# Which of two arena places a set of weight sums is formed in first, and when its stores are issued

## The chip, the core and the metric

The kernel runs on one core of one Trainium2 chip. The core has a matrix engine (PE), a vector engine (DVE), a scalar engine (ACT), a general engine (POOL) and SP, which here only issues DMAs. POOL and ACT issue DMAs too. Each engine runs its own instruction list strictly in order and waits at semaphores for the others; a transfer issued by SP, ACT or POOL goes through that engine's own DMA queue, and all queues share the core's 16 DMA engines.

The metric is the device time of one execution in microseconds (us), as the median over several runs. Beside it stands one execution taken with the hardware profiler, whose trace all readings of engines come from.

## The reference

```python
x = A_x                                            # [1, 2048, 1024] bf16
g = _sigmoid((x * gate_w).sum(-1, keepdims=True))
a = _A_ref(x, A_wqkv, A_wo)     # 32 heads of 32, each position attends to 8 positions, 2 apart
b = _B_ref(x, B_w_gate, B_w_up, B_w_down)          # gelu(x Wg) * (x Wu), 3584 wide, then Wdown
return g * a + (1 - g) * b
...
def _B_ref(x, w_gate, w_up, w_down):
    g = jnp.einsum("bsd,df->bsf", x, w_gate)
    u = jnp.einsum("bsd,df->bsf", x, w_up)
    h = _gelu(g) * u
    return jnp.einsum("bsf,fd->bsd", h, w_down)
```

Almost all work is matrix products: x by the 3072 columns of wqkv, x by 7168 columns of gate and up weights, and the last product, in which the down projection and the attention's output projection are taken together (their rows are stacked).

## The kernel before

**Products by halves.** Every product is done as a 2 by 2 block product with seven block multiplications in place of eight (Winograd's form of Strassen's scheme). That needs sums and differences of the blocks of both factors. They are formed by DVE, in bf16, before PE uses them. For the last product the sums of the right factor (rows of `B_w_down` and `A_wo`, 18 slices of 128 rows by 512 columns for each quarter) are called T1 to T4. They do not fit into the on-chip memory (SBUF) during the first part of the kernel, so they are formed early, in nine *sets* of two slices, and stored to the DRAM tensors `t_d[0..3]`. The last product loads them back from 511 us on.

**One arena.** Nearly all of SBUF is one tile, `arena`, cut by hand into places given in KB of a partition. A place is used for one thing after another. Those that matter here:

- 92 to 108 (`R_W0`): the raw gate and up weights of the first pairs (`raw_ab`), read by PE and by DVE's sums (L327) in the first 24 us. 92 to 100 is later a set's place.
- 56 to 72 (`R_XN`, later `R_PR`): first x as loaded (`xn`, whose second half is 64 to 72), which PE transposes by 16.4 us; later four of the six tiles that take the products of q and k (`prod_tile`, `pr_off = 56, 60, 84, 64, 68, 88`). The diff's title calls 64 to 72 the place of the q-k tiles.
- `R_TF`: where each of the nine sets lies. A set takes 8 KB: four tiles of two slices, `r11, r12, r21, r22`.

**A set's life.** `tf_load(q)` (L873) has SP load the four tiles (eight DMAs of 256 KB for sets 0 and 1 together, L877). `t_forms` (L881) has DVE form the sums in place: one instruction of 128x2048 (L892) gives r11 and r12, and two of 128x1024 (L895) give r22 and then r21. Then POOL issues four stores of 256 KB to `t_d` (L898). Sets 0 and 1 are loaded right behind the kernel's head, ahead of 16 DMA transposes of the second half of x (L1343), all on SP.

**The order of DVE's work.** `t_forms` is a Python generator, one of many background tasks. The main loop goes over *units* b (28 matmuls of 128x512 each, 6.05 us): PE's groups p1, p73 of the unit before, p5, possibly the queued reduces (`slotq`), p26, p4 of the unit before. Between p73 and p4, DVE adds a partial product to two banks (L400) and PE's p4 writes one of them again, so that L400 must end before p4 begins. At the end of a unit `run_bg` spends a budget of about 4.7 us on tasks, by priority: a task is resumed, issues its instructions up to its next `yield`, and the number that it yields is taken off the budget. What a generator holds behind its last `yield` is issued only when it is resumed once more, which may be in a later unit. `t_forms` has the lowest priority of those tasks (6).

**q and k.** From unit Q0 = 2 on, the units are those of q and k. Each stores a part of its result through POOL (L523, L524). Two units later `qk_prods` (L612) forms three product tiles: one DVE instruction of 128x4096 for two tiles (L599) and one of 128x2048 for the third (L592). The first q-k unit's go to 56, 60 and 84, the second's to 64, 68 and 88. PE reduces the six with 24 matmuls (L604). The other lines that come up: L207, the sums of the second half of x, which need the DMA transposes; L245 and L251, a product of gate and up parts and its store by POOL; L289 to L298, the gate's sigmoid, with POOL's load of `zc` and DVE's sum of it (L291).

**POOL's queue.** POOL works off its DMA issues in order. Its DMAs use eight semaphores in turn, so that each issue also waits for the landing of the eighth one before it.

Of the kernel before, what the change touches and what calls it, by code (L numbers as in the profile page):

```python
# [46 lines left out]
R_ST = 178  # L47
R_P5B = 198.5
R_RAW = (0, 8)
R_TF = (92, 64, 100, 108, 92, 16, 92, 100, 108)  # L50
R_S = (16, 24)
R_O = (36, 32)
R_VB = (40, 48.25)
# [9 lines left out]
def _win_ap(src: bass.AP, dims):  # L63
    return AP(src.tensor, src.offset, [list(src.ap[0])] + [list(d) for d in dims])
# [3 lines left out]
def kernel(  # L68
# [12 lines left out]
    nc = tc.nc  # L81
# [24 lines left out]
    def reg3(kb, a, b):  # L106
        return reg(kb, a * b).rearrange("p (a b) -> p a b", a=a)
# [19 lines left out]
    t_d = [tc.dram_tile([P, NK, SC], BF16, name=f"t_d{k}") for k in range(4)]  # L127
# [9 lines left out]
    with tc.manual_schedule(engines={mybir.EngineType.PE, mybir.EngineType.DVE, mybir.EngineType.Activation,  # L137
# [63 lines left out]
        def flat(a):  # L201
            return a.rearrange("p a b -> p (a b)")
# [661 lines left out]
        NP = 2  # L864
# [5 lines left out]
        def tf_set(q):  # L870
            return [reg3(R_TF[q] + NP * k, NP, SC) for k in range(4)]

# [8 lines left out]
        def t_forms():  # L881
            for q in range(NQ):
                tf_q[0] = q
                if q in (N1, N2):
                    tft.prio = 3.9 if q == N1 else 4.5
                    tasks.sort(key=lambda t_: t_.prio)
                while now[0] < (Q0 + (0, 1, 4, 6, 7)[q] if q < N1 else 1 + (TB if q < N2 else TC)):
                    yield None
                r11, r12, r21, r22 = tf_set(q)
                n_ = NP * SC  # L890
                both = _win_ap(flat(r11), [[n_, 2], [1, n_]])
                TT(out=both, in0=_win_ap(flat(r12), [[2 * n_, 2], [1, n_]]), in1=both, op=ALU.subtract)  # L892
                yield 1.14
                for o_, a, b_ in ((r22, r22, r11), (r21, r21, r22)):
                    TT(out=flat(o_), in0=flat(a), in1=flat(b_), op=ALU.subtract)  # L895
                    yield 0.61
                for k, t in enumerate((r11, r22, r12, r21)):
                    nc.gpsimd.dma_start(out=t_d[k][:, NP * q:NP * q + NP, :], in_=t)  # L898

        for q, b in ((2, 2), (3, 4), (4, 5)):  # L900
            at(Q0 + b, lambda q=q: tf_load(q))
        at(TB, lambda: ([tf_load(q) for q in range(N1, N2)], spill_load(1)))
        at(TC, lambda: [tf_load(q) for q in range(N2, NQ)])
        tft = bg(t_forms(), 6, Q0)

        def tf_done():
# [495 lines left out]
```

## Time and profile before

| what | us |
|---|---|
| median of 3 runs (lowest, highest) | 718.88 (717.62, 720.47) |
| the profiled execution | 717.67 |
| its span, first to last instruction | 715.8 |
| PE busy in the span | 705.9 |
| DVE busy | 671.6 |
| ACT busy | 330.0 |
| PE busy in 60 to 72 us | 10.18 of 12 |
| DVE busy in 50 to 60 us | 5.24 of 10 |
| mean share of the DMA engines busy in 50 to 60 us | 1.04 |
| granted TensorE clock | 1.00 throughout |

The span is cut into instructions of each engine; "busy" is the sum of their durations. In a time line each row is one instruction, or some alike in a row (x4): start, length, engine, line, operation, output and inputs; in brackets, the engine's idle time just before and what ended it. The share of the DMA engines is a mean over 16 and can read a little over one.

### The profile page before, as it was taken

Reading aid. Unit: us, or ns where it says so; the run is one execution under the profiler, and the core shown is the slowest. Engines: PE = TensorE matmul, PEld = TensorE weight load, DVE = VectorE, ACT = ScalarE, POOL = GpSimd, SP = SyncE. Lnnn points to the kernel's source line nnn. Section 1 sums busy time; section 2 is a strip of 40 time slices with the busy share of each in tenths; the row PEclk is TensorE's granted clock in tenths of the full one; section 3 lists DMA queues with packets and bytes.
Section 4 is the critical chain, followed back from the end, with each engine's and each line's share of the span. In section 5 each row is a group of like instructions: output and inputs, shape, how many; then the busy total and the mean of one; then the engine's idle time right before and its main releaser. Section 6 shows DMA issues by size and latency. Waiting matters only on the chain.

```text
span 715.8 us, 10650 instructions
## 1 busy us (share of the span) xinstructions
PE 705.9 (99%) x4033; PEld 407.7 (57%) x4089; DVE 671.6 (94%) x631; ACT 330.0 (46%) x602; POOL 143.9 (20%) x248
## 2 busy tenths in 40 slices
PE   9999999999999999999999999999999999999998
PEld 4465656655544444444444444444447886758887
DVE  3997989989999999999999999999699899799997
ACT  5554446445466565555555555555322321132431
POOL 1243544322512332121300010101110002100011
PEclk9999999999999999999999999999999999999999
DMA  9979352384484768665763763464950799995951
GB/s 300 320 197 294 135 177 65 97 239 141 143 278 145 246 206 250 207 218 182 235 180 105 264 208 126 159 261 137 423 241 36 298 397 399 412 430 232 396 215 60
DMA packets 94755, 162.03 MB, mean 226 GB/s; under 512 B 23680, under 2 KB 71200, under 8 KB 90352
## 3 DMA queue, kind: packets, MB, share of 16 engines
q1 hardware_dynamic: 77632, 105.46, 42.9%
q0 software_dynamic: 16352, 48.29, 19.5%
q10 hardware_dynamic: 720, 7.60, 2.7%
q8 instruction: 32, 0.52, 0.3%
q14 instruction: 19, 0.16, 0.1%
HBM read 112.17 MB, written 54.14 MB: 232 GB/s over the span
## 4 chain that ended last, share of the span: by engine, by line
PE 91%; DVE 3%; DMA 3%; issue 2%; POOL 0%; ACT 0%; DVEq 0%; POOLq 0%
PE banks L354 62%; PE banks L1073 19%; PE banks L1106 7%; PE banks L604 2%; DMA h_d<-arena 1%; DMA arena<-h_d 1%; DVE arena L400 1%; PE banks L150 0%; DMA gblk<-g_d 0%; DVE arena L314 0%; DVE arena L774 0%; DVE arena L768 0%; ACT arena L224 0%; POOL gblk L305 0%; PE banks L218 0%
## 5 line engine op out<-in xcount | busy, mean ns | idle before, releaser
L354 PE MATMUL banks<-arena 128*128 128x512 bf16 x2191 | 484.9, 379 | 4.7 <-DVE arena L400 1.5
L354 PEld LDWEIGHTS <-arena 128*128 128x128 bf16 x2240 | 245.8, 110 | 241.6 <-issue 8.2
L1073 PE MATMUL banks<-arena 128*128 128x256 bf16 x1260 | 138.3, 273 | 0.0
L1073 PEld LDWEIGHTS <-arena 128*128 128x128 bf16 x1260 | 123.3, 98 | 15.2 <-issue 0.3
L381 ACT COPY arena<-banks 128x512 f32<-128x512 f32 x80 | 46.9, 587 | 129.8 <-PE banks L354 129.8
L400 DVE TENSOR_TENSOR arena<-banks,arena 128x1024 bf16<-128x1024 f32 x80 | 97.4, 1219 | 8.9 <-ACT arena L408 3.6
L362 ACT CAST arena<-banks 128x512 bf16<-128x512 f32 x104 | 60.9, 585 | 44.1 <-PE banks L354 43.8
L768 DVE TENSOR_TENSOR arena<-arena 128x4096 bf16<-128x4096 bf16 (+1 forms) x40 | 73.5, 1859 | 0.3
L774 DVE TENSOR_TENSOR arena<-arena 128x2048 bf16<-128x2048 bf16 (+2 forms) x53 | 68.0, 1282 | 1.0
L251 POOL DMA_DIRECT2D h_d<-arena x28 | 20.4, 731 | 216.0 <-DVE arena L245 142.1
L1106 PE MATMUL banks<-arena 128*128 128x512 bf16 x281 | 62.6, 379 | 0.5
L389 ACT COPY banks<-banks 128x512 f32<-128x512 f32 x80 | 45.6, 570 | 23.3 <-PE banks L354 20.1
L1031 DVE TENSOR_TENSOR arena<-arena 128x2304 bf16<-128x2304 bf16 x40 | 53.3, 1352 | 0.5
L599 DVE TENSOR_TENSOR arena<-arena 128x4096 bf16<-128x4096 bf16 x22 | 50.1, 2284 | 3.9 <-DMA t_d<-arena 3.8
L376 ACT COPY banks<-banks 128x512 f32<-128x512 f32 x80 | 46.1, 576 | 14.1 <-PE banks L354 12.9
L1078 ACT COPY banks<-banks 128x256 f32<-128x256 f32 x60 | 21.4, 356 | 61.7 <-PE banks L1073 61.5
L1106 PEld LDWEIGHTS <-arena 128*128 128x128 bf16 x288 | 28.0, 98 | 34.0 <-DMA arena<-h_d 0.6
L360 ACT ACTIVATE arena<-banks 128x512 bf16<-128x512 f32 x56 | 33.4, 597 | 20.1 <-PE banks L354 20.1
L954 DVE TENSOR_TENSOR arena<-arena 128x2048 bf16<-128x2048 bf16 (+1 forms) x40 | 41.8, 1112 | 0.4 <-DMA arena<-h_d 0.4
L1039 DVE TENSOR_TENSOR arena<-arena 128x2304 bf16<-128x2304 bf16 x28 | 37.7, 1352 | 0.2
L245 DVE TENSOR_TENSOR arena<-arena 128x2048 bf16<-128x2048 bf16 x28 | 34.0, 1216 | 2.8 <-ACT arena L362 2.8
L314 DVE TENSOR_TENSOR arena<-arena 128x1024 bf16<-128x1024 bf16 x56 | 36.1, 686 | 0.5
(92 smaller groups left out, 455.5 us busy)
## 6 DMA issues: line engine op xcount, KB each, us to landing
arena<-t_d SPq DMA_DIRECT2D x8, 2304.0 KB, 10.2
h_d<-arena POOLq DMA_DIRECT2D x28, 512.0 KB, 4.7
arena<-w_c SPq DMA_DIRECT2D x12, 1152.0 KB, 13.5
t_d<-arena POOLq DMA_DIRECT2D x36, 256.0 KB, 5.3
arena<-h_d SPq DMA_DIRECT2D x6, 1536.0 KB, 13.0
arena<-in_B_w_down_dram SPq DMA_DIRECT2D x28, 256.0 KB, 6.1
r_d<-arena ACTq DMA_DIRECT2D x3, 2304.0 KB, 9.0
arena<-r_d SPq DMA_DIRECT2D x3, 2304.0 KB, 14.2
```

Of the source, the lines that this page charges most:

```text
L354: self.pe = nc.tensor.matmul(ps, lhsT=self.L[form](kt), rhs=rhs[:, kt, :], start=(start and kt == 0), stop=(kt == HK - 1), skip_group_chec ...
L362: nc.scalar.copy(out=o_, in_=i_)
L376: nc.scalar.copy(out=self.Y, in_=self.X)
L381: nc.scalar.copy(out=self.p5s, in_=self.V)
L389: nc.scalar.copy(out=self.Z, in_=self.Y)
L400: TT(out=self.T[:, :, c2s], in0=pair, in1=self.p5s.rearrange("p (o n) -> p o n", o=1).to_broadcast([P, 2, SC]), op=ALU.add)
L599: TT(out=dst, in0=_win_ap(q, [[sq, 2], [0, NWIN], [1, AC]]), in1=_win_ap(k, [[sk, 2], [-DIL, NWIN], [1, AC]]), op=ALU.mult)
L768: TT(out=prod2[:, t % 4:t % 4 + m, :], in0=flat(ab).rearrange("p (o n) -> p o n", o=1).to_broadcast([P, m, NWIN * AC]), in1=_win_ap(v[:, t ...
L774: TT(out=h(0) if w > 1 else o_[:, t:t + m, :], in0=h(0), in1=h(1), op=ALU.add)
L1031: TT(out=o_, in0=a, in1=b_, op=op)
L1073: nc.tensor.matmul(c(i, h, j), lhsT=l[:, kt, j * P:(j + 1) * P], rhs=r[:, kt, :], start=False, stop=(kt == KH - 1), skip_group_check=True)
L1106: nc.tensor.matmul(ps, lhsT=L[:, i, j * P:(j + 1) * P], rhs=R[:, i, :], start=(start and q == 0), stop=(q == NK - 1), skip_group_check=not ...
```

## The change

The places of sets 0 and 1 change places in `R_TF`: set 0 now lies at 64 (the q-k tiles' place) and set 1 at 92. And in `t_forms` the four stores of a set are issued directly behind its last difference, ahead of the last `yield` of the generator's round and not behind it.

```diff
-R_TF = (92, 64, 100, 108, 92, 16, 92, 100, 108)
+R_TF = (64, 92, 100, 108, 92, 16, 92, 100, 108)
...
                 for o_, a, b_ in ((r22, r22, r11), (r21, r21, r22)):
                     TT(out=flat(o_), in0=flat(a), in1=flat(b_), op=ALU.subtract)
+                    if o_ is r21:
+                        for k, t in enumerate((r11, r22, r12, r21)):
+                            nc.gpsimd.dma_start(out=t_d[k][:, NP * q:NP * q + NP, :], in_=t)
                     yield 0.61
-                for k, t in enumerate((r11, r22, r12, r21)):
-                    nc.gpsimd.dma_start(out=t_d[k][:, NP * q:NP * q + NP, :], in_=t)
```

The instruction lists of PE, DVE, ACT and SP keep their order. On POOL, the four stores of set 0 come ahead of the q and k stores of the first q-k unit (they were behind them, behind the load of `zc` and behind two stores of L251), and those of set 1 come to where those of set 0 were, ahead of the second unit's q and k stores. The stores of sets 2 to 8 stay where they were in POOL's list. Which semaphores are waited for changes with it, for the same data.

## The prediction

> **What bounds the kernel now.** I read the page's first part, then the waits, then the stretch of time in which the change acts on PE, DVE, POOL and the SP queue.
>
> ```profile
> span 715.8 us, 10650 instructions
> PE 705.9 (99%) x4033; PEld 407.7 (57%) x4089; DVE 671.6 (94%) x631; ACT 330.0 (46%) x602; POOL 143.9 (20%) x248
> ```
>
> PE is busy all but 9.9 us, and the chain that ended last is 91% PE. Only what fills an idle stretch of PE can pay. The list of waits (us in total, times, longest) has one DVE wait on a DMA and two on which PE pays for a late DVE:
>
> ```profile
> DVE arena L599 <- DMA t_d<-arena: 3.8, 1, 3.8
> PE banks L354 <- DVE arena L400: 1.5, 2, 1.2
> PE banks L604 <- DVE arena L592: 0.5, 1, 0.5
> ```
>
> The time line of DVE (start, length, instruction, idle before and its releaser) shows where the first lies:
>
> ```profile
> 49.01 0.19 DVE L291 TENSOR_REDUCE zs<-zc 128x8 f32<-128x32 f32 x1
> ...
> 53.54 1.23 DVE L400 TENSOR_TENSOR arena<-banks,arena 128x1024 bf16<-128x1024 f32 x1 [1.00 <-PE banks L354]
> 54.68 0.23 DVE L296 TENSOR_SCALAR go<-zs 128x8 bf16<-128x8 f32 x2
> 58.67 2.29 DVE L599 TENSOR_TENSOR arena<-arena 128x4096 bf16<-128x4096 bf16 x1 [3.76 <-DMA t_d<-arena]
> 60.88 1.22 DVE L592 TENSOR_TENSOR arena<-arena 128x2048 bf16<-128x2048 bf16 x1
> 62.02 1.22 DVE L207 TENSOR_TENSOR arena<-arena 128x2048 bf16<-128x2048 bf16 x1
> 63.15 1.22 DVE L400 TENSOR_TENSOR arena<-banks,arena 128x1024 bf16<-128x1024 f32 x1
> ...
> 70.60 1.22 DVE L400 TENSOR_TENSOR arena<-banks,arena 128x1024 bf16<-128x1024 f32 x1
> ```
>
> The L599 at 58.67 writes the second q-k unit's products to the place of set 1, so it waits until set 1 is stored. Everything behind it on DVE is late, and PE's time line shows the bill:
>
> ```profile
> 60.27 1.36 PE L604 MATMUL banks<-arena,ones_r 128*32 128x512 bf16 x20
> 62.15 0.40 PE L604 MATMUL banks<-arena,ones_r 128*32 128x512 bf16 x4 [0.52 <-DVE arena L592]
> 62.48 8.14 PE L354 MATMUL banks<-arena 128*128 128x512 bf16 x35
> 71.87 4.48 PE L354 MATMUL banks<-arena 128*128 128x512 bf16 x20 [1.25 <-DVE arena L400]
> ```
>
> Why the store is late is on POOL's time line: set 0 (L898, four stores) goes out at 46.61 though its last difference ended at 41.97, and set 1 only behind the next q and k stores.
>
> ```profile
> 46.61 2.36 POOL L898 DMA_DIRECT2D t_d<-arena  x4
> 49.39 0.55 POOL L523 DMA_DIRECT2D q_d<-arena  x1 [0.42 <-DVE zs L291]
> 49.92 0.54 POOL L524 DMA_DIRECT2D k_d<-arena  x1
> 50.45 0.54 POOL L898 DMA_DIRECT2D t_d<-arena  x1
> 51.56 0.54 POOL L898 DMA_DIRECT2D t_d<-arena  x1 [0.57 <-DMA h_d<-arena]
> 52.43 0.54 POOL L898 DMA_DIRECT2D t_d<-arena  x1 [0.32 <-DMA t_d<-arena]
> 53.30 0.54 POOL L898 DMA_DIRECT2D t_d<-arena  x1 [0.33 <-DMA t_d<-arena]
> ```
>
> The last is issued at 53.30, such stores land in 5.0 to 5.7 us there (the view of t_d in that stretch), and 58.5 is when L599 is let go.
>
> **The change part by part.** No instruction is added or removed, and the order of instructions on PE, DVE, ACT and SP stays. On POOL alone two groups move: set 0's four stores to ahead of the first q and k stores, set 1's to where set 0's were. The later sets keep their places.
>
> *The removed wait.* The place that L599 needs is now set 0's. POOL stood idle from 21.9 to 43.4, so the four stores go out as their DVE results come: from 40.6 (L892 at 39.30 lasts 1.22) to about 42.9. At the longest landing seen for these stores between 46 and 50 (6.4 us) they are home by 49, 6 us before DVE reaches L599 at 54.91. So the 3.76 us go. Each part alone nearly does it: with only the places swapped, set 0 would leave at 46.61 to 48.97 and land by 54.6; with only the stores moved, set 1 would leave from about 46.6 to 49.4 and land by 55.8, a wait of at most 0.9.
>
> *What PE gets of it.* The reduces at 60.27 need L592, which would now end at 58.3. An undisturbed group of 24 such reduces takes 1.41 (the one from 104.44 to 105.85), here 62.48 - 60.27 = 2.21, so 0.80 is gained. The profile calls 0.52 of it idle. For the second gap I walk DVE: after L599 at 54.91, L592 at 57.1, L207 at 58.25, and L400 at 59.4. Its PE input comes one unit (28 matmuls of 0.216, 6.05 us) after the 53.54 of the one before, at 59.6. From one L400 to the next DVE needs 70.60 - 63.15 = 7.45, so the next runs from 67.05 to 68.3. PE wants it where its idle time begins now, 71.87 - 1.25 = 70.62, less the 0.80 already gained: 69.82. It is there 1.5 us ahead, so the 1.25 goes too. Sum: 0.80 + 1.25 = 2.05, with the idle figures 0.52 + 1.25 = 1.77. I take 2.0; bounds 0 and 2.05 of this part.
>
> *The swapped loads on SP.* Set 0's loads now need only xn's second half, free at 16.4 when the transposes on PE end; before they waited for L327 until 22.25. Set 1's take that wait over. No engine gains: the queue is full there (DMA share 1.06 from 18 to 27 us). The four A_wqkv loads ahead end at 28.2 (the last issue at 14.0 and the longest landing, 14.2), and eight loads of 256 KB land behind them from 28.95 to 34.04 whenever they were issued. Set 0 is used at 39.30, set 1 at 45.29, so 5 us cover it. If the earlier 1 MB were served among the A_wqkv loads, it would take 2.7 us at the 385 GB/s of that stretch, and L460 at 31.36 needs the last but one of those; I take nothing. The place at 92 is loaded again for set 4 at 62 to 64 us, long after set 1's stores.
>
> *What stands behind the moved stores on POOL.* Four issues of 0.54 to 0.76 end by 43.7 at the latest against 43.40 for the first q store: up to 0.3 later. Then comes the load of zc, for which DVE waits at L291 (49.01). It landed in 2.9 us; the q store that ran behind four t_d stores took 5.5. Issued at 44.6 to 44.9 it lands between 47.5 and 50.4, so L291 is between on time and 1.4 late. Cover: DVE's 1.00 idle before L400 at 53.54, and the 12 matmuls (2.6 us) between that unit's p73 and its p4 less the 1.23 of L400, together 2.4. So nothing; without that cover 1.4. The second h store waits for set 0's first to land (47 at the latest, 0.9 late), for which no engine waits.
>
> *The shared DMA engines.* The DMA transposes of x run from 28.94 on SP; L207 needs the last. Their steps are 1.3 us, but not the last two:
>
> ```profile
> 48.69 2.87 SPq L1343 DMA_TRANSPOSE arena<-in_A_x_dram  x1
> 51.61 2.96 SPq L1343 DMA_TRANSPOSE arena<-in_A_x_dram  x1
> 54.61 1.31 SPq L877 DMA_DIRECT2D arena<-in_B_w_down_dram  x1
> ```
>
> They were slow while 3 MB of h and t_d stores drained. The last landed at 51.61 + 7.0 = 58.6, 0.4 after DVE could now begin L207, so L207 starts at 58.7 and the next two L400 are 0.25 later than walked; 1.2 of cover is left. The same bytes drain earlier, so I take the landing as unchanged. Bounds: up to 2 us earlier, for the queue had room from 40 on, which gains nothing; or 4.7 later (the last rival).
>
> The Trainium skill speaks against moving stores into the transposes' time: "DMA: Bandwidth & Descriptors", section "Queues, rings and completion order", says that each DMA engine takes turns packet by packet between the queues that have work. The trace agrees with that, by the steps of 2.9 against 1.3. By the rule alone the moved megabyte delays the transposes it now meets, which is the last rival.
>
> Sum: the profiled execution took 717.67 (span 715.8 and 1.87 around it), so 715.7 after it. The runs' median is 718.88, 1.21 above; carried over, **716.9**.
>
> **Rivals.** (a) *The gain is eaten further on*: PE is 2 us ahead, but a later stretch follows something else. For it: DVE is busy 218.2 of 220 us from 260 to 480, and PE waits on L400 again at 248.31 (0.23). Against it: DVE's idle times up to there (1.76 at 150.73, 0.36 at 165.97) wait for PE, so DVE moves along; no later wait of PE is on a DMA. Time 718.9. (b) *It doesn't do what it says*: the wait only changes its releaser, L599 now held for set 0's bytes. That needs landings of 14 us from 40.6; the longest store seen there took 6.4. Also 718.9. (c) *Slower*: the early megabyte stretches the transposes from 41 on and the later two megabytes stretch the last ones as before. 3 MB drained from 45.3 to 58.6, 225 GB/s, so 1 MB is 4.7 us: the last transpose lands at 63.3, L207 holds DVE until then, L400 ends at 65.6 where PE needs it at 63.4 (reduces end at 61.68, eight matmuls), 2.2 lost; the next ends 7.45 later at 73.1 against 69.82 + 2.2, 1.1 more. 3.3 against the 2.05 now: 1.3 slower, 720.2. It decides from a last landing of about 62.0 on; from 60.0 it already costs. Against it: SP's step at 54.61 shows the slowing was there already.
>
> **How the numbers follow.** Forecast 0.66, (a) and (b) together 0.20, (c) 0.09, and 0.05 for a stall that I have not seen, above 722.5. The runs before lie from 717.62 to 720.47, so 0.5% (3.6 us) is what one can tell from no change. The forecast's 2.0 lies inside it: faster by more needs 715.3 or less, which no idle time of PE between 20 and 500 us pays for, only scatter: 0.14. Slower by more: the last case and the end of (c), 0.07. Range: 1.9 below the forecast for scatter, and up to (c): 715.0 to 720.4.
>
> **What would show it.** Right: no wait of L599 on t_d; the reduces near 60.3 in one group of 24 and no idle PE before the L354 that stands at 71.87; set 0's stores from 40.6; L207 near 58.7. Wrong: DVE idle before L291 (zc), or before L207 beyond 60.0 (transposes), or PE's total idle still near 9.9.

## The result and the profile after

The changed kernel takes 715.19 us (median of 7 runs, 714.86 to 716.73) against 717.92 (7 runs, 717.33 to 720.47) for the kernel before, beside which it ran. The ratio is 0.9957, with a 95% interval of 0.9943 to 0.9972: faster by 2.0 to 4.1 us. The forecast was 716.9, a gain of 2.0 on the 718.88 of the three runs known then. The direction and the place were right. The size was too small: the two medians lie 2.7 us apart, and the ratio means 3.1.

The first part of the page of the kernel after:

```profile
span 713.3 us, 10651 instructions
PE 704.4 (99%) x4033; PEld 406.9 (57%) x4089; DVE 671.6 (94%) x631; ACT 329.9 (46%) x602; POOL 143.5 (20%) x248
```

The span is 2.5 us shorter and PE's work is the same. The time line of DVE in the stretch of the change (start, length, instruction, idle before and its releaser):

```profile
49.16 0.21 DVE L291 TENSOR_REDUCE zs<-zc 128x8 f32<-128x32 f32 x1
49.28 2.28 DVE L599 TENSOR_TENSOR arena<-arena 128x4096 bf16<-128x4096 bf16 x1
53.31 1.23 DVE L592 TENSOR_TENSOR arena<-arena 128x2048 bf16<-128x2048 bf16 x1 [1.75 <-DMA h_d<-arena]
54.45 1.22 DVE L400 TENSOR_TENSOR arena<-banks,arena 128x1024 bf16<-128x1024 f32 x1
55.59 0.24 DVE L296 TENSOR_SCALAR go<-zs 128x8 bf16<-128x8 f32 x2
55.73 2.29 DVE L599 TENSOR_TENSOR arena<-arena 128x4096 bf16<-128x4096 bf16 x1
...
59.07 1.22 DVE L207 TENSOR_TENSOR arena<-arena 128x2048 bf16<-128x2048 bf16 x1
60.20 1.22 DVE L400 TENSOR_TENSOR arena<-banks,arena 128x1024 bf16<-128x1024 f32 x1
...
67.65 1.23 DVE L400 TENSOR_TENSOR arena<-banks,arena 128x1024 bf16<-128x1024 f32 x1
```

The wait of the second L599 on t_d is gone: L599 starts at 55.73, not 58.67. But a wait has come that was not there, 1.75 us of the first L592 on an h store. It took the place of the 1.00 us in which DVE had waited for PE. PE's time line:

```profile
60.39 1.48 PE L604 MATMUL banks<-arena,ones_r 128*32 128x512 bf16 x24
61.80 12.31 PE L354 MATMUL banks<-arena 128*128 128x512 bf16 x55
74.04 1.48 PE L604 MATMUL banks<-arena,ones_r 128*32 128x512 bf16 x24
```

The 24 reduces run in one group and no idle time stands before the next 56 matmuls (55 recorded). And POOL's, where set 0 now leaves at 40.93 and set 1 at 46.93:

```profile
40.93 0.57 POOL L898 DMA_DIRECT2D t_d<-arena  x1 [18.92 <-DVE arena L892]
41.66 1.61 POOL L898 DMA_DIRECT2D t_d<-arena  x3 [0.16 <-issue]
...
44.58 0.77 POOL L289 DMA_DIRECT2D zc<-z_d  x1
45.34 1.49 POOL L251 DMA_DIRECT2D h_d<-arena  x2
46.93 0.56 POOL L898 DMA_DIRECT2D t_d<-arena  x1
47.65 1.72 POOL L898 DMA_DIRECT2D t_d<-arena  x3 [0.17 <-issue]
```

zc and the two h stores are issued when they were before, but with 1 MB of set 0 ahead of them in the queue. zc landed in 4.6 us (2.9 before), the h stores in 6.2 and 7.3 (3.8 and 5.3 before).

**Where the time went.** All kernels here issue the same matmuls, so one measure serves for all: the starts of PE's matmuls at a few landmarks. From the second group of reduces to the last product's first matmul (L1106 in the kernel before) there are 434.8 us in both kernels, and from the first L1073 to the last matmul 168.83 and 168.82. Only three stretches differ: up to the first reduces, from the first to the second group of reduces (the *stage*), and the L1106 near 525 us. The stage took 16.01 us and takes 13.65: 2.36 of the 2.5. Another 0.27 was a wait ahead of an L1106 at 526, which the kernel after does not have, and its first reduces begin 0.12 later, from the kernel's head.

### The profile page after: what moved, and what is told of

It reads as the page before. It is cut to its first block, busy times and chain, and to the rows that moved or that the text cites. A ratio compares the mean times of both kernels' runs of the same rounds, so it can differ in the third digit from the quotient of the medians.

```text
span 713.3 us, 10651 instructions
## 1 busy us (share of the span) xinstructions
PE 704.4 (99%) x4033; PEld 406.9 (57%) x4089; DVE 671.6 (94%) x631; ACT 329.9 (46%) x602; POOL 143.5 (20%) x248
## 4 chain that ended last, share of the span: by engine, by line
PE 95%; DVE 3%; issue 1%; DMA 1%; SPq 0%; DVEq 0%
PE banks L354 65%; PE banks L1074 19%; PE banks L1107 9%; PE banks L604 2%; DVE arena L400 1%; DMA arena<-in_A_x_dram 1%; DVE arena L314 0%; DVE arena L774 0%; DVE arena L222 0%; DVE arena L768 0%; PE banks L273 0%; DVE arena L1288 0%; DVE arena L248 0%; DVE arena L892 0%; DVE arena L245 0%
## 5 line engine op out<-in xcount | busy, mean ns | idle before, releaser
L400 DVE TENSOR_TENSOR arena<-banks,arena 128x1024 bf16<-128x1024 f32 x80 | 97.5, 1219 | 7.9 <-ACT arena L408 3.6
L251 POOL DMA_DIRECT2D h_d<-arena x28 | 20.3, 729 | 216.4 <-DVE arena L245 142.6
L376 ACT COPY banks<-banks 128x512 f32<-128x512 f32 x80 | 46.1, 576 | 14.4 <-PE banks L354 13.2
L599 DVE TENSOR_TENSOR arena<-arena 128x4096 bf16<-128x4096 bf16 x22 | 50.1, 2284 | 0.1
```

The lines of the kernel that those rows point to most:

```text
L376: nc.scalar.copy(out=self.Y, in_=self.X)
L400: TT(out=self.T[:, :, c2s], in0=pair, in1=self.p5s.rearrange("p (o n) -> p o n", o=1).to_broadcast([P, 2, SC]), op=ALU.add)
L599: TT(out=dst, in0=_win_ap(q, [[sq, 2], [0, NWIN], [1, AC]]), in1=_win_ap(k, [[sk, 2], [-DIL, NWIN], [1, AC]]), op=ALU.mult)
```

## The experiments

Theory A: PE pays for nothing but how late DVE is behind the second L599. The rivals are named with the runs. The indented passages are what was expected, written before each run.

**1. Each part of the change alone.** The exchange of places without moved stores (swap_only), and the moved stores without the exchange (move_only):

```diff
swap_only, against the kernel before
-R_TF = (92, 64, 100, 108, 92, 16, 92, 100, 108)
+R_TF = (64, 92, 100, 108, 92, 16, 92, 100, 108)
move_only, against the changed kernel
-R_TF = (64, 92, 100, 108, 92, 16, 92, 100, 108)
+R_TF = (92, 64, 100, 108, 92, 16, 92, 100, 108)
```

> Only the two places are exchanged; the stores of a set stay behind the generator's last yield. Theory A (PE pays for nothing but DVE's lateness behind the second L599): L599 finds set 0 stored long before, starts at 54.9, no wait of L592 either, and from PE's first group of 24 reduces (near 60.3) to its second group there are 13.65 us, as in the changed kernel (16.01 before). Span 713.0 to 713.6. Theory B (a part of the gain comes from the stores being issued earlier, on the DMA queues): between 13.65 and 16.01, and a span over 714.

> Only the stores are moved ahead of the last yield; set 0 stays at 92 and set 1 in the q-k tiles' place. Theory A: set 1's stores leave from 46.9 and land by about 56.2, L592 waits some 1.8 us for the h store as in the changed kernel, the second L599 starts at 55.7 to 56.4, early enough (up to 56.5) for PE not to wait: 13.65 us between the two groups of reduces, span 713.0 to 713.7. Theory B: a part of the gain only, span over 714.

Measured: swap_only 715.34 us (6 runs), ratio 0.9955 (0.9944 to 0.9967), span 713.3, stage 13.65. move_only 716.45 us (12 runs), ratio 0.997 (0.9956 to 0.9984), span 714.6, stage 14.11. So the exchange alone did all of it in this execution, as theory A had it. Two things were closer than expected: L592 waited 0.81 us for h, and set 0's last store landed at 54.80, only 0.2 us ahead of L599 (55.02). move_only fell short of it. Its stage and span are what theory B had, but theory B's reason, stores that go out earlier, is ruled out by swap_only, which moves no store and has all of the gain. The DVE of move_only shows another reason:

```profile
50.61 0.21 DVE L291 TENSOR_REDUCE zs<-zc 128x8 f32<-128x32 f32 x1 [1.53 <-DMA zc<-z_d]
...
54.08 1.22 DVE L592 TENSOR_TENSOR arena<-arena 128x2048 bf16<-128x2048 bf16 x1 [1.06 <-DMA h_d<-arena]
...
57.47 2.29 DVE L599 TENSOR_TENSOR arena<-arena 128x4096 bf16<-128x4096 bf16 x1 [0.88 <-DMA t_d<-arena]
```

zc came late behind set 0's bytes, then h, then set 1's own landing: three waits where the expectation had one. L599 began at 57.47, past the 56.5 from which PE has to wait.

**2. The wait replaced by work.** With the places exchanged, DVE forms the third product tile of the second q-k unit once (dose_1) or three times (dose_3) more, ahead of L599. No transfer is touched.

```diff
             a = 0
+            for _ in range(3 if (s, t) == (0, 1) else 0):
+                qk_mult(out_[2], u.T[:, 0, 2 * AC:3 * AC], u.T[:, 1, 2 * AC:3 * AC])
             while a < ND:
```

> The places exchanged as in swap_only, and DVE forms the third product tile of the second q-k unit once more ahead of L599, 1.14 us of DVE work with no DMA in it. Theory A: DVE has 1.55 us to spare, PE none the worse: 13.65 us between the two groups of reduces. Theory B says the same.

> As dose_1, with the tile formed three times more: 3.42 us of DVE work in the place of the 3.76 us wait of the kernel before. Theory A: PE loses 3.42 - 1.55 = 1.87 (15.5 us between the two groups of reduces), most of the 2.36 that the kernel before loses there, and the span is 1.9 longer than swap_only's. Theory B: no loss, since no transfer is later.

Measured: dose_1 has a stage of 13.65 and a span of 713.6. dose_3 has 15.73, a loss of 2.08 against the 1.87 expected, and a span of 716.4. Its DVE and its PE:

```profile
54.98 3.73 DVE L592 TENSOR_TENSOR arena<-arena 128x2048 bf16<-128x2048 bf16 x3
58.63 2.28 DVE L599 TENSOR_TENSOR arena<-arena 128x4096 bf16<-128x4096 bf16 x1
```

```profile
62.10 0.40 PE L604 MATMUL banks<-arena,ones_r 128*32 128x512 bf16 x4 [0.41 <-DVE arena L592]
62.43 8.14 PE L354 MATMUL banks<-arena 128*128 128x512 bf16 x35
71.74 4.48 PE L354 MATMUL banks<-arena 128*128 128x512 bf16 x20 [1.17 <-DVE arena L400]
```

The same two stalls as in the kernel before, with no DMA wait of L599. The lateness of L599 is enough to make the loss; no late transfer is needed for it. Against swap_only, L599 began 3.61 later (58.63 - 55.02) and 3.61 - 1.55 = 2.06: the walk of the prediction holds, and the dose was a little larger than planned. The span grew by 3.1, not 1.9, since an L1106 near 526 also waited 1.03 us.

**3. The two kernels again, unchanged.** The timed runs of before spread over 3.1 us, those of after over 1.9. Is the profiled execution of before a typical one?

> The kernel before once more, unchanged, for a second look at how long its DVE wait is. Theory A (the profiled execution of before was a cheap one, since the landing of set 1's last store scatters): the wait of the second L599 on t_d differs from 3.76 us by some tenths to over 1 us, most likely longer, and PE's time between its first two groups of 24 reduces lies between 15.7 and 17.5 with it, following the wait one for one. Theory C (what was missed of the gain lies elsewhere, in the wait of L1106 on h at 525 us): 16.0 again within 0.15, and another wait there.

> As before_2: Theory A has the wait of L599 on t_d between 3.3 and 5 us and PE's loss following it; Theory C has 3.76 within 0.15.

> The changed kernel once more, unchanged. Both theories: 13.65 us between the first two groups of reduces, within 0.1, since nothing that PE needs there hangs on a transfer with less than 0.5 us to spare. Theory C adds: the gap ahead of the L1106 near 523 us, 0 in the first look, is again 0 to 0.1; Theory A lets it scatter up to 1 us as in the other kernels.

> As after_2: 13.65 us between the first two groups of reduces, within 0.1. The wait of L592 on h_d (1.75 in the first look) scatters by up to 1 us, without a cost to PE as long as the L400 behind it begins within 1.4 us of its input.

Measured: the wait of L599 was 5.52 in before_2 and 3.94 in before_3, the stage 17.91 and 16.19, the spans 717.5 and 716.5. Theory A held in the main: against the first profile the wait grew by 1.76 and 0.18, the stage by 1.90 and 0.18, and the first profile was the cheapest of the three. But 17.91 is above the 17.5 expected, and theory C has a share: of the 0.7 us by which the span of before_3 is longer, 0.48 is the L1106. From before_2, DVE and PE:

```profile
60.53 2.29 DVE L599 TENSOR_TENSOR arena<-arena 128x4096 bf16<-128x4096 bf16 x1 [5.52 <-DMA t_d<-arena]
```

```profile
62.88 0.61 PE L604 MATMUL banks<-arena,ones_r 128*32 128x512 bf16 x8 [1.68 <-DVE arena L599]
64.02 0.40 PE L604 MATMUL banks<-arena,ones_r 128*32 128x512 bf16 x4 [0.52 <-DVE arena L592]
64.35 13.99 PE L354 MATMUL banks<-arena 128*128 128x512 bf16 x55
```

Behind the reduces the L400 stall of the first profile (1.25 us idle) is missing, and yet the 55 matmuls take 13.99 us, against 12.31 in the changed kernel. From 65.08 to 68.47 eight of them start 0.40 to 0.43 us apart and not 0.216: PE ran at half speed there (granted clock 0.51 from 65 to 68.5), which cost 1.66 us (last section). The L400 ended at 73.68 and PE came to it at 73.86, so this loss stands in the place of the stall, not on top of it.

The changed kernel has 13.65 both times, but after_2 has lost time before the stage. Its span is 714.2, and its DVE shows:

```profile
50.98 0.21 DVE L291 TENSOR_REDUCE zs<-zc 128x8 f32<-128x32 f32 x1 [1.40 <-DMA zc<-z_d]
...
54.57 1.23 DVE L592 TENSOR_TENSOR arena<-arena 128x2048 bf16<-128x2048 bf16 x1 [1.18 <-DMA h_d<-arena]
```

Both waits together use up DVE's cover: one matmul there starts 0.846 us behind the one before and not 0.216, so PE lost 0.63. The expectation spoke of the stage alone, where nothing had less than 0.5 us to spare, and there it held. Ahead of the stage there was less.

**4. Have the moved stores a price?** The changed kernel and the exchange alone, timed on one chip, and the changed kernel with set 0 stored twice:

```diff
stores_twice, against the changed kernel
-                    if o_ is r21:
+                    for _ in range((2 if q == 0 else 1) if o_ is r21 else 0):
                         for k, t in enumerate((r11, r22, r12, r21)):
```

> The changed kernel, timed beside the next one on the same chip. Theory D (the moved stores have a price of their own: set 0's bytes go ahead of the load of zc and of the h stores, DVE waits at L291 or L592, and in some executions PE pays up to 0.7 us before its first reduces; the exchange of places alone has all the gain): 715.3 to 715.9, a median 0.1 to 0.6 above swap_timed. Theory E (the moved stores cost nothing): the same median within 0.1.

> The places alone exchanged, timed beside the changed kernel. Theory D: 715.0 to 715.5, first reduces near 60.4, 13.65 us to the second group, no wait of L291. Theory E: the same as the changed kernel.

> The changed kernel with the four stores of set 0 issued twice, so that 2 MB and not 1 MB go ahead of the load of zc and the two h stores. Theory D: zc and h land some 4 to 5 us later, L291 and the first L592 wait 5 us or more together where the changed kernel waits 1.3 to 2.6, DVE's cover there (2.4) is used up, and PE's first reduces begin at 62.5 to 65 and not at 60.4, while the 13.65 us behind them stay within 0.5; span 715.5 to 718.5. Theory E: first reduces at 61 at the latest, span under 714.3.

Measured: after_timed 715.98 us (6 runs, 714.95 to 716.23), swap_timed 716.04 (6 runs, 715.12 to 716.67); ratios 0.9962 (0.9946 to 0.9977) and 0.9963 (0.9948 to 0.9977). The medians lie 0.06 apart, as theory E had it and not the 0.1 to 0.6 of theory D; a difference well under 1 us could not be told from these runs. Theory D's statement that the exchange alone has nothing to lose is refuted by swap_timed's own profile (DVE, then PE):

```profile
57.29 2.29 DVE L599 TENSOR_TENSOR arena<-arena 128x4096 bf16<-128x4096 bf16 x1 [2.23 <-DMA t_d<-arena]
```

```profile
70.42 4.48 PE L354 MATMUL banks<-arena 128*128 128x512 bf16 x20 [0.61 <-DVE arena L400]
```

Stored as late as before, set 0 itself can land too late: its stage is 14.42. So each part removes most of the wait and leaves another transfer with little to spare: zc and h with the moved stores, set 0 with the exchange alone.

stores_twice took 721.28 us (one run), span 719.5, over the expected 718.5. Its DVE, then its PE:

```profile
54.70 0.21 DVE L291 TENSOR_REDUCE zs<-zc 128x8 f32<-128x32 f32 x1 [5.53 <-DMA zc<-z_d]
```

```profile
55.79 1.89 PE L354 MATMUL banks<-arena 128*128 128x512 bf16 x8 [1.42 <-ACT banks L376]
60.52 6.12 PE L354 MATMUL banks<-arena 128*128 128x512 bf16 x20 [2.85 <-DVE arena L400]
```

That PE pays once the cover is gone is shown: the first reduces came at 66.57 (theory E had 61 at the latest), the stage behind them took 13.65. But it was not the second megabyte in the queue that made zc late. POOL's time line:

```profile
44.97 0.54 POOL L898 DMA_DIRECT2D t_d<-arena  x1 [1.75 <-DMA t_d<-arena]
...
49.89 0.77 POOL L289 DMA_DIRECT2D zc<-z_d  x1
```

zc was issued 5.3 us later than in the changed kernel (44.58), since POOL had four more stores to issue and waited for landings between them. Once issued it landed in 4.79 us, hardly more than the 4.56 there. So this run prices a late zc and not bytes ahead of it. That the moved stores cost nothing in any execution is refuted by after_2 and move_only, where PE lost 0.63 and 0.64 ahead of the reduces; in the median the two kernels do not differ. New in stores_twice are ACT's part (its tanh waits for L291 too, and L376 stands behind it) and what the 2.85 us did to PE's clock (last section).

**5. Set 0 behind zc and ahead of h.** An order meant to give zc and set 0 enough room at once:

```diff
 nc.gpsimd.dma_start(out=zc[:], in_=z_d[:, ts].rearrange("g (p i) -> p g i", i=ZI))
+while behind_zc:
+    behind_zc.pop(0)()            # set 0's four stores
...
                     if o_ is r21:
+                        if q == 0:
+                            behind_zc.append(store)
+                        else:
+                            store()
```

> The changed kernel, but set 0's four stores are issued right behind the load of zc and ahead of the two h stores; set 1's stay behind its last difference. Theory D (each of the two parts alone leaves one transfer with too little to spare: zc where the stores come first, set 0's own landing where they come late): here zc lands in 2.9 to 3.7 us and L291 doesn't wait, L592 waits 1 to 2.2 us for h, the second L599 starts by 56.3 and doesn't wait for t_d, so PE's first reduces begin at 60.2 to 60.5 and the second group follows 13.65 us later; most times lie at 715.0 to 715.4, as the better executions of the changed kernel, and few at 716. Theory E (the spread of the times has nothing to do with this stretch): median 715.9, with times at 715 and at 716 as before.

Measured: 720.14 us (12 runs, 717.3 to 722.89), ratio 1.0024 (1.0009 to 1.0039): slower than the kernel before. zc landed in 2.9 us and L291 did not wait, as expected, and the stage took 13.65; but the h stores left at 48.20, not 45.34, and DVE and PE show the rest:

```profile
56.43 1.23 DVE L595 TENSOR_TENSOR arena<-arena 128x2048 bf16<-128x2048 bf16 x1 [4.27 <-DMA h_d<-arena]
```

```profile
58.84 4.48 PE L357 MATMUL banks<-arena 128*128 128x512 bf16 x20 [2.07 <-DVE arena L403]
```

(L595 is L592 of the other kernels, L403 their L400.) The expectation had 1 to 2.2 us of wait for h and missed by 2. It counted the megabyte ahead of h but not the 2.9 us by which h is issued later. The profile explains its own execution, one of the three shortest of the 12, and not the median. In eight of the twelve the granted clock is lower, 0.995 to 0.998, and they took 719.16 to 722.89; the four with 0.999 or 1.0 took 717.3 to 718.75. So stretches at half speed, as in before_2 and stores_twice, are the likely rest; no such execution of this kernel was profiled. Of the tried orders, the changed kernel's and the exchange alone are the best, and nothing tells them apart.

**All profiles together** (us; waits of DVE, and what PE loses, the matmuls' starts compared with their undisturbed pitch of 0.216):

| kernel | L291 on zc | L592 on h | L599 on t_d | PE, ahead of the reduces | stage | PE, L1106 | span |
|---|---|---|---|---|---|---|---|
| before | 0 | 0 | 3.76 | 0 | 16.01 | 0.27 | 715.8 |
| before_2 | 0 | 0.66 | 5.52 | 0 | 17.91 | 0.06 | 717.5 |
| before_3 | 0 | 0 | 3.94 | 0 | 16.19 | 0.75 | 716.5 |
| after | 0 | 1.75 | 0 | 0 | 13.65 | 0 | 713.3 |
| after_2 | 1.40 | 1.18 | 0 | 0.63 | 13.65 | 0 | 714.2 |
| after_3 | 0 | 1.31 | 0 | 0 | 13.65 | 0 | 713.4 |
| after_timed | 0.29 | 1.08 | 0 | 0 | 13.65 | 0 | 713.2 |
| swap_only | 0 | 0.81 | 0 | 0 | 13.65 | 0.12 | 713.3 |
| swap_timed | 0 | 0.88 | 2.23 | 0 | 14.42 | 0.10 | 714.2 |
| move_only | 1.53 | 1.06 | 0.88 | 0.64 | 14.11 | 0.40 | 714.6 |
| dose_1 | 0 | 0 | (work) | 0 | 13.65 | 0 | 713.6 |
| dose_3 | 0 | 0.49 | (work) | 0 | 15.73 | 1.03 | 716.4 |
| stores_twice | 5.53 | 1.01 | 0 | 6.23 | 13.65 | 0.01 | 719.5 |
| behind_zc | 0 | 4.27 | 0 | 2.23 | 13.65 | 0 | 716.1 |

One line fits the stage in all rows to 0.2 us: take x, the start of the second L599 less that of the first reduces. With x under -3.9 the stage is 13.65, and above it grows by x + 3.9. For the kernel before, x = 58.67 - 60.27 = -1.60 gives 2.30 (measured 2.36); before_2, +0.16, gives 4.06 (4.26); dose_3, -1.79, gives 2.11 (2.08); swap_timed, -3.12, gives 0.78 (0.77); move_only, -3.42, gives 0.48 (0.46); after, at -4.66, none. The largest miss, 0.2, is before_2, whose PE ran at half speed for a while. The walk of the prediction put the same bound at 1.5 us behind an L599 at 54.91, which is -3.86.

## Why the prediction fell short

**Right.** The mechanism is shown: the DVE wait made L599 late, L599's lateness alone makes PE's loss (dose_3), and with the wait gone the stage runs undisturbed in every profile of the changed kernel. The points to watch that the prediction named for a right outcome came: no wait on t_d, one group of 24 reduces at 60.39, no idle time behind it, set 0's stores from 40.93, L207 at 59.07 (58.7 forecast). The last transpose landed at 53.62 + 4.9 = 58.5 (58.6 taken), so the slower rival (c) did not come, nor did (b). Rival (a) is refuted: the 434.8 us behind the stage are the same.

**The term that was mis-sized: the gain of PE in the stage, 2.05, taken from one execution.** It was too small for two reasons.

First, the idle times were read as the profile gives them. An idle time counts from the modelled end of a matmul, which lies 0.379 us behind its start, while undisturbed matmuls start every 0.216. A stall so costs 0.16 more than its idle figure, and one under 0.16 shows none. From start to start, the 1.25 of the L400 was 1.627 - 0.216 = 1.41. The prediction had corrected the first stall in this way (0.80, not 0.52), but not the second. And there was a third: at 64.42 a matmul began 0.368 behind the one before, when the L400 from 63.15 ended (64.38), which is 0.15 without any idle time in the list. 0.80 + 0.15 + 1.41 = 2.36, as measured, above the 2.05 that the prediction gave as the upper bound of this part.

Second, the profiled execution was carried over to the median by a constant 1.21. That came from three runs. Over the seven of the result the median of before stands 0.25 above its profile, that of the changed kernel 0.12. And what is removed is not a constant: the wait was 3.76, 5.52 and 3.94 in the three profiles of before, and the profile that was priced had the shortest. The mean stage of before is 16.70, 3.05 above 13.65. The L1106 adds 0.36 in the mean, and the first reduces of the changed kernel begin 0.33 later, which leaves 3.08. The spans of the three profiles of before average 716.6, those of the four of after 713.5: 3.1 apart, which is what the ratio of the timed runs says (0.43% of 717.9). A wait on a DMA scatters with the DMA, so to remove it gains more in the usual execution than in the cheapest. Three profiles are few for the size of this, and the wait is not all that scatters: of the 17 runs of the kernel before that were timed beside swap_only, the three with a granted clock of 0.998 are the three longest (720.25 to 720.64; the rest 717.69 to 719.66).

In parts, the forecast was 1.71 too high: 0.63 in the profiled execution (715.7 foreseen, 715.07 measured) and 1.09 in the constant.

The prediction also took 0.5% (3.6 us), read from the spread of three runs, as what can be told from no change, and saw its gain inside that. The seven runs of each kernel gave a ratio between 0.9943 and 0.9972, so the gain is told from no change.

**Wrong, though it did not decide the time.** "For which no engine waits" was said of the second h store. The first L592 writes over what that store reads, and waited 1.75, 1.18, 1.31 and 1.08 us for it in the four profiles. The prediction followed the moved stores to zc and not to the next one behind it. The cover it had worked out for zc (2.4 us) served for h as well, so PE paid nothing in three of the four. "So nothing", for zc, held in three of four too: with 1.40 on zc and 1.18 on h the cover was gone and PE lost 0.63. And the landing of set 0 with the places alone swapped, put at 54.6 from the one execution, was 54.80 in swap_only and 57.07 in swap_timed.

**Not told by the prediction: the L1106.** PE waited there between 0.06 and 0.75 us in the three profiles of before, 0.10 to 1.03 in four of the edited kernels, and not at all in the four of after. Where it is long enough to be listed, it is a wait on the late loads of h. Why the changed kernel is free of it was not tried; it may be chance, and it is worth 0.4 at most in the mean.

## What to carry to other kernels

A store whose place is written again is a wait on the DMA queue that scatters. Measure such a wait in several executions before pricing its removal, and take PE's loss from matmul start to matmul start, not from the idle column. When stores move ahead in a queue, follow every transfer behind them to the instruction that waits for it, loads and stores alike: here a megabyte moved by some places turned one DVE wait into smaller ones on two other transfers, and the next such move (behind zc) made the kernel slower than it began.

## What was unexpected of the hardware

After 2.85 us without a matmul, PE came back at half speed. The windows of stores_twice (length, then busy time and count of each engine, granted clock, DMA share, GB/s):

```profile
57.50:60.50 3.00, 0.18 (x1) 0.00 (x0) 2.39 (x4) 0.00 (x0) 0.00 (x0) 0.99 1.06 416
60.50:64.00 3.50, 3.48 (x9) 1.40 (x9) 3.50 (x5) 1.37 (x4) 2.12 (x4) 0.52 1.06 365
64.00:66.50 2.50, 2.50 (x13) 1.48 (x11) 1.70 (x2) 0.57 (x1) 0.00 (x0) 1.00 1.09 363
```

The granted clock is 0.52 from 60.5 to 64, and eight matmuls start 0.38 to 0.43 us apart and not 0.216, which costs 1.64 us on top of the idle time. In before_2 the same came after less: gaps of 1.68 and 0.52 us with eight reduces (0.61 us) between them, then the half speed from 65.08 on. But after 1.42 us of idle time in stores_twice, and after 2.07 in behind_zc, the pitch was 0.216 at once. The Trainium skill, "TensorE: Matmul & The Clock Gate", Part 1, has the clock fall to half after an idle window of some 3.4 us that runs freely, and asks for no idle gaps above that. These gaps were shorter; the measurement says that 2.85 can be enough, and that two shorter ones close together can. The length of a gap alone does not tell the cases here apart, and what does was not tried.

The other finding is how much longer a transfer takes with a megabyte of stores ahead of it in POOL's queue: the 16 KB load of zc landed in 2.7 to 3.6 us where no t_d store went ahead of it (before and its repeats, the exchange alone, behind_zc) and in 4.6 to 6.1 behind 1 MB of them (the changed kernel, move_only). The later of the two 512 KB h stores landed in 5.1 to 6.3 us without those stores ahead of it and in 7.0 to 8.2 with them (here behind_zc too). With 2 MB ahead, issued 5.3 us later, the two took 4.8 and 6.8 (stores_twice). Whether the order in the queue makes this or the DMA engines that all queues share was not tried.
